# First pair's k and q staged in f32 through the sync queue, with a new table of order and engines

## The chip, the cores and the metric

One NeuronCore of one Trainium2 chip runs the whole program. The metric is the device time of one execution in microseconds; lower is better. Five runs of the kernel before gave 199.79 to 201.91 us with a median of 200.88. The profile is of one further execution, which took 201.26 us.

## The reference

q, k and v are f32 of shape (batch 4, heads 8, 768 positions, head dim 64). Attention looks only at the six best chunks of 32 keys for each query; the result goes through a gated MLP. In short:

```python
k_min, k_max = k_chunks.min(3), k_chunks.max(3)      # 24 chunks of 32 keys
ub = sum(maximum(q * k_min, q * k_max))              # bound per query and chunk
ub = where(causal, ub, -1e9); top_chunks = argsort(ub)[..., -6:]
scores = where(selected and causal, scale * q @ k.T, -1e9)
attn = softmax(scores); x = attn @ v                 # heads side by side: 512 wide
h = relu(x @ w_in); u, v = halves of h
v_n = (v - mean(v)) / sqrt(var(v) + 1e-6)
v_s = w_spatial @ v_n + b_spatial
out = (u * v_s) @ w_out
```

## The kernel before

The heads are worked in 16 pairs (two heads of 64 fill the 128 partitions), four pairs to a batch. For each pair:

- *Load.* k, q and v come from DRAM by DMAs that POOL issues. They cast from f32 to f16 on the way, into `kp`, `qs` and `vt`. The k and q of the first pair come in halves, one head each (lines 364 and 369).
- *Prepare* (`prep_ops`, and `prep_first` for pair 0). k is transposed to `kT`, either by TensorE with a copy out of PSUM, or by a transposing DMA on SP's queue. VectorE takes maximum and minimum over each chunk (`t`, then `kmm`). Copies spread these into `km`, and `kT` into `kh`. q is transposed on TensorE and split in its positive and negative part (`rq`). A matmul of `rq` and `km` gives the bounds (line 475). VectorE masks, takes the eight best, and writes a selection beside q in `qs`. That is transposed to `a`, by TensorE or by a transposing DMA (line 502).
- *Attend.* The score matmuls (line 627) take `kh` and `a`. The exponential on ScalarE writes `e` (line 637). The causal diagonal is masked by an added matmul or by POOL. The matmul with v (line 653) is followed by a normalisation into `x16` and a transpose into `xT`.

After four pairs the MLP of a batch runs: v and u (lines 699 and 726), the normalisation, the spatial matmul (740), the gate `g`, its transpose `gT`, the output matmul (761), a copy `o`, and a store on SP's queue.

`Schedule.op` records every operation with the engines that may do it, what it reads and writes, and for some a choice: `s.choice` names two alternatives, of which the plan takes one, as for a transpose on TensorE or by DMA. The order isn't found when the program is built. The string `PLAN` holds three characters for each operation: which one, on which engine, and in which PSUM bank its result goes. `Schedule.run` reads it and emits the operations in that order. Each engine then takes its own instructions strictly in that order, and so do the queues of SP and POOL: an instruction whose input isn't there holds all that stand behind it. All matmul results share eight PSUM banks.

The cost figures beside an operation (`("POOL", 0.81, 0)`) belong to the search that wrote the table; the program doesn't act on them.

Of the kernel before, what the change touches and what calls it, by code (L numbers as in the profile page):

```python
# [8 lines left out]
F32 = mybir.dt.float32  # L9
# [5 lines left out]
P = 128  # L15
# [20 lines left out]
def blocks(groups):  # L36
# [13 lines left out]
    "0A00600400500300700D00200F00Q00H00C00E00000900a00c00B00100I00L00d00f40K10+82600P10G01AC0g00/00i0"  # L50
    "0b00O01003Q00h00N00q02804k00M00o10k01201101402701912AG1710rK0j01300m00l01501C11B12B01612D02E0181"
    "0s00J00p11DO1E02F03US0n10t10uW1F02N20v01G02Q20w03R02G00x01H42I03S00y82H03V13X02P22O24oC0e04m03Y0"
    "3Z00803a01I12L22K24l02RG2M21sK8400W01yO0X03lS4p03c03b00z12T11hW2J20V02S01u03n03i11a41nC1p02U84r0"
    "1XG1+01j02V01JK1vC1L03d03e04t04s01UO2W04u01c09O03m01MW1W03g03j11kK3f02X05341x01PO1m01O04v01R03h1"
    "2ZS2b888C5404w04z21Z02a03oK2c01rW4y22jS2rO1T82002uG2l05013k18911e03p05503q02105212g42dS3AC3r03tK"
    "1f02202w05118B04x22t04+02f01g02908503u08D03vG3w035W3GO2i02/S8C03D88602443T04/156K3C03F041C5709P0"
    "25037031062G6486309Q06503xW3I032458043049S4MG8E066O3405909S84B09T02oCAi03+48G03z039S3K03L04PK8F0"
    "6702q04UW4O04n04a84R09V05DC4005E05BG5C10T04JO4c08PK8J02n44CC2y05QG8H03M09W04L046S8K08I05j84W08Q0"
    "4E08M10U04804XO8R05l09X05S05TK4TW8SCC005IS4Z02z05K09Z02+09Y05L48T09a09j89f145G4G00R05oO9h14e00S0"
    "68S8U09e09l04H08V09k05N05F44I09d08ZC8a05V08N15uK8O15q05H05d84f05gO5f0Aj08XG5W49b28L05Y0691Ak05PC"  # L60
    "4g0Am88Y0FA0C109c25a05r45b06AW5i09mG5t094SAn05w03OO4i89C45c09n09R03P06B18cC9509o05nK5y09g15z09p0"
    "9q05+0A+09i1Ap09D0A/18fO99WAq0C208g08704j0C4S6Y48+G8iO8d06iK60C6109A08j0Ar06EW8/0C516OO9186F06P0"
    "8tGB02As06Z06G08qC6JS6K0At09206a0Au0C70FB0C808nW8k0C90CB08r0Aw08u06Q16H0CA09F8Az1B14B30Ay0Ax06j0"
    "Av18o06dO9G0A0C9wG6I06L0A8WB20A10AI89x0CH18v0CC0AOSAP06M0FG0FC0B44B506CC6D06k0B606e0CLGCN0A5S6vC"
    "6w0A906sKGU0AJ06/W0Z0B70FI06f0CG16x0CE0AT86R0CM16N06S09z4A60CF0B80AWOAX06t0FH09+0700CD06u0COC6g0"
    "ALG8lSFJ06yOFK06b06z0CP09H0Ho0AU0960FM0CQ06+097475KAM06T06l06U00Y0J60CR08w06h0FL0AB8AC0AZOAa0760"
    "72G9I06c06V0770730A20710BtCBc8Bu0BEOBF0A3KGV0AQ06m06n09J07406W09K0AD08x0Bd0ARW6o0AE08y06X0FQ16p0"
    "BnCAF0AG07cOFN0FO0Bo07I4BqGFVSBr0Ab0Ac0CJ1BP8CS0BiC7d0Bj06r0FX0FW1BHGCK1CI17J0BI078KAd0FU26q0Ga0"
    "790BQ0FP0FYCBfSBg0FR1BKG7K0Ae0BL07e0FT1FS1CYWGW0FZ0D087A0Fa0CZ0CeSD107L0CjG7S4Fb0CmCAl0Gb0Hu07f0"
    "Ck0Gn1CpW7B0Gd07T0Cn07m87U0C30Cq0BSOCf0Fc0Go0CbGCwCHp0BM0Bk07V0DBKHw0BT07n0Hv0Cc0BVWBW09MS7W0CzO"  # L70
    "Gf0C+0Cx0Bv0Gc0Ge0Gg0Gj1Gp4Gl1BlGD5WGi1BX07C0Gr0Bw0Gq1Hx07wO7x0DC0Hq09N0BNCBx0BY07o0Cr0Hz0Hy07M0"
    "Cg0D60BZ0FtKGL4D8WBa0GM07y0Gk0Gh0Fu0ChSD90Cs0Gs4G7CAf0H+0I42By0GFKFlWFm0GG0Ct0Cu0I207ZGGt0DD0Gu0"
    "Gv07a0D20FwSD3WDE07FKG80FiGMG0DF0Fx0DG0G44DIC7p0B+WI7SDJ07z0JA8DoC7G0DPKJ80G50Gw0FD0Fo4GAOGm1B/0"
    "JB1I90DQ0J70GIW7H0Dp0Fj0DR1JE0GB0Dy8Dz0E8GDS0DKOJD0I01I61I81JG0DL0H3KI31JF0H/0Fp0Dq0FzSGJ0De4DM0"
    "D+1Hr0I51HHCMM0JI0I10IAWGC0MI0HI0JH0HZ8JK0E90H40GN0Ha0Df0Dg0HEODN0IB0IC0DUCJM2DV0HBKHF0Hc8F+0MH0"
    "EA0ID0GX0HC0H04DO0DW1F/0DX0MO0Hd0H10HOWJJ0JROEBSDjCDk0Dl0JN1GDGJS0HP0JL0H6KGO0IE0MY17g0EC0ED0JT0"
    "JU8MN07+0H70Dh0DY0E2O7P4HJ0E30E40Na0D/CGP0DT0DZ07q0Dm0HUWFq0MP0GQ0JV0Ou0MQ07Q0Dn0HV0JP1E00JW0Dr0"
    "JO0E5SHRKHS0Ds0IiGIj0IQODa0JX0E10E60Nc0Iz4FrWG00E71Di0Dt0Du0Db0MR0I+0Hf881KJQ1MbGDc0Hg0ItSH80H9C"
    "Md0Hh0HW0Mc1Iu0G10Ma17j4Iw8Dv0Dx0Dd0INGIR0EYSHK0EEODw0Ix0IO07R08207t8JY0IVGNg0G20HXWIW0MX1HL0EZ0"
    "IbKIc0MZ1MS0MU1O+0MT1MV1Ea07k1EF0JpGMW07u0HM0Eb0Me4K6KJq0Mf0Mg0Nb0Mh0K70IKCJh8EG0EH0K3SNi0Ji0EOG"  # L80
    "JsKIl8EP0Hi0KE4IL0I/0IoCEiOEQ0Im0Nh0Ow0P00Nj0Nl0J90Nk0Nm0No1Jt0Jk8Ip0Ej0Ek0Mi0K0KKF0ER0Hj0IS0Hk0"
    "Ov0Jl0K40JvCNv4Jw0P20Nx1QE0O/0P10Iq0Ir8JeSEI0GR0Nw0IYGIZ0F0CQC0K10J00Nn0EsWJ10Id0Et0Jf0P40KHGJ20"
    "Np1KB4ITKIe0KC0KI0Jm0P30K80MrSMs0NA8Mu4Mv0P91NDGHl0If0NE0Eu0PDSPF1Jx0P60El0Nr0Nq1Ig0PE0KJ0NB0J30"
    "P82JnONs17b0Mz4Jy0F10M+0Nt2Nu2K9GN3KKK0ELSNG8Ev0N0WNy4Jz0J+0KL0F20N10KM0P50P70PGOKOGNz0N+0NH0N40"
    "QD0KkWN/0ES0KP1PH0QI0Ka8PC2KQKNO4NRGNS0KR0Kb0PI0PJ0KS0Kc0N50KT0KU0KpGKd0Kq0NP0O00F30NLOKl0EM0Ke0"
    "KuKL58Mo4QJ0Kv0MJ0KVSL60KW0Kr07l0L8GQXC830Km0QL0PK0NM0PB1QK0Mp0L70QN0KX0QZ1Kw1QM0QO0L2WL30Kn0QP0"
    "QR0Kx0L40QU1NT0OlOOm0Em0Ew0LE4OXKPA0LF0LG0Oa8Ky0OUSKY0OV0Ob0NI0OiWL90OY0OKOQY0EV4Ec0KZ0OCCNJSQQ0"
    "EN0ON8QS2OfKOL0Og0NU0LA1Kf0O9GKs0EW1OA0Mw0NV0QaONW0Nd0Mx4N60Oj0O6KLBSQb0Kg0PhGPi07v0N70N80Ko0Qc0"
    "LC0Kt0LD0OD0LHWQd0Ox0Pb4Kz0PoGQT0Ki0Pc0LI0Pp0EzSLJ1OO0PzOEfCPQ4Kh0O70OHGOc0Kj0E+1Q08Qe0PTWEpKK+0"
    "OI0OE0OFGPR0OdSEg1F40P+0K/0On0Oo0QF0Eq0OP0Op0QV1E/0Q10Le4PeCPf0OQ0LUOPU0L00NX0Pj0Oq0Q3KQ/8Q40LV0"  # L90
    "QqCR00PuSPv0QW0QnWPWKLf0OR0Pr8L10RHSQo0OS0R6GPs0LW0LoWPw0Lg0RN8RI0PX0Lp0Lq0PY0QvSLX0LKOLL0Qr0RKK"
    "Lh0R70Q50LM0LN0Er0RL0QyCOr0Ly4PZGPk0Pl0Pm0Eh0RO0RP0LY0Qz0LO0Qw0R10QkKQl0RC8R9OPxCQs0Q60Q70Q80M6S"
    "EX0RD0Lr0RA0RE0RWGQtKR20R30R40Rq8RFOM70RQ0RR0Lz0Q90M80LRCRS0RUWRgKM90L+0R+ORV0Rr0Rh0Ri0Rj0RX0R/0"
    "S00Rk0RY0S10RvSLi0LlWRZ0Rw0Rx0Ra0Rs0SHKRbORc0Rd1Re0F7GRf0Ry0SBSLb8LS0Lc0S8CS90L/0Rl0Rz0Ls0Rm0Rt0"
    "SC0SEOLT0S20Ru0SK8SL0Lv4Rn0SD0Ro0Rp0MA0SI0F80S30S40S60SF0S50SQST2GF90S70SM0TC8Lm0Ln0Ld0M00SA0SaW"
    "SR0SS0ST0SuCT30Sb0Lw0Sc0SU0SJ0Sd0Se0Sk4Sv0T40Sw0SNKM3SLx0Sl0Sm0SG0MDOSx0Sy0T50SXWT60Sn0TD0ME0MF0"
    "SO0SP0ShCTE0SY1SZ0SpGM40Si0M50S/4T9OT00TA0Sj0T10TF0THWSq0SrKSs0TB0TI0TJSSt0TK0TL0"
# [20 lines left out]
class Schedule:  # L118
# [7 lines left out]
    def op(self, alts, emit, key, r=(), w=(), take=None, drop=None, load=0.0, tag="", when=None):  # L126

        o = Op()
        o.alts = {e: (occ, vis) for e, occ, vis in (alts if isinstance(alts, list) else [alts])}
        o.emit, o.take, o.n, o.when = emit, take, len(self.ops), when  # L130
        deps = set()
# [47 lines left out]
def pe_cost(ns):  # L179
    occ = sum(n * MM + 0.0027 for n in ns)  # L180
    return occ, occ + 0.22
# [11 lines left out]
def kernel(  # L193
# [11 lines left out]
    nc = tc.nc  # L205
    B, H, S, D = q.shape
# [4 lines left out]
    NQT = S // P  # L211
# [15 lines left out]
    V0 = 0.2  # L227
# [30 lines left out]
    KH = [("DVE", 0.36, 0.44), ("POOL", 0.47, 0.53), ("ACT", 0.41, 0.55)]  # L258
    KM = [("POOL", 0.24, 0.30), ("DVE", 0.18, 0.30), ("ACT", 0.11, 0.26)]

    def ring(n, shape, dt, name):
        return [cp.tile(shape, dt, name=f"{name}{j}") for j in range(n)]
# [14 lines left out]
    v_r = ring(4, [P, 2, NQT, D + 2], F16, "vt")  # L277
    kT_r = ring(2, [P, S], F16, "kT")
# [70 lines left out]

    PAIRB = P * 2 * NQT * D * 2 / 120e3  # L350

    def load_ops(i, key):
        b, hp = divmod(i, HP)

        def view(a):
            return a[b, 2 * hp:2 * hp + 2].rearrange("h (so si) d -> si h so d", si=P)

        def one(a, hi):
            return a[b, 2 * hp + hi].rearrange("(so si) d -> si so d", si=P)

        kp, qs, vt = kp_r[i % len(kp_r)], qs_r[i % len(qs_r)], v_r[i % len(v_r)]
        def load_q(hi, key):
            c0 = D * (1 - hi)
            s.op(("POOL", 0.81, 0), lambda: nc.gpsimd.dma_start(out=qs[:, :, hi, c0:c0 + D], in_=one(q, hi)), key,  # L364
                 w=[("qd", i % len(qs_r), hi)], load=PAIRB / 2, tag=f"ldq{i}")

        if i == 0:
            for hi in range(2):
                s.op(("POOL", 0.81, 0), lambda hi=hi: nc.gpsimd.dma_start(out=kp[:, hi], in_=one(k, hi)), key + 0.2 * hi,
                     w=[("kp0", hi)], load=PAIRB / 2, tag=f"ldk{i}")  # L370
                load_q(hi, key + 0.2 * hi + 0.1)
        else:
            s.op(("POOL", 1.0, 0), lambda: nc.gpsimd.dma_start(out=kp, in_=view(k)), key,  # L373
                 w=[("kp", i % len(kp_r))], load=PAIRB, tag=f"ldk{i}")
            for hi in range(2):
                load_q(hi, key + 0.1)
        s.op(("POOL", 1.0, 0), lambda: nc.gpsimd.dma_start(out=vt[:, :, :, 0:D], in_=view(v)), key + (0.2 if i else V0),  # L377
             w=[("vd", i % len(v_r))], load=PAIRB, tag=f"ldv{i}")

# [37 lines left out]
    def prep_ops(i, key):  # L417
# [3 lines left out]
        bk = Bank("tr")  # L421
# [394 lines left out]
```

## Time and profile before

| | us |
|---|---|
| median of 5 runs | 200.88 |
| lowest and highest | 199.79, 201.91 |
| the profiled execution | 201.26 |
| its span, from first to last instruction | 199.6 |
| TensorE busy (matmuls) | 183.2, 92% of the span |
| VectorE busy | 156.6, 78% |
| ScalarE busy | 151.3, 76% |
| POOL busy (its DMA issues counted) | 121.2, 61% |
| first matmul, first score matmul, start of the last group of matmuls | 4.66, 15.63, 194.20 |

The rows of issued DMAs on the page (operation, count, size of each, median time from issue to landing) that bear on the change:

```profile
out_dram<-o SPq DMA_DIRECT2D x24, 256.0 KB, 2.7
qs<-in_q_dram POOLq DMA_DIRECT2D x32, 96.0 KB, 5.0
...
kp<-in_k_dram POOLq DMA_DIRECT2D x15, 192.0 KB, 5.5
```

The page is read as follows. PE is TensorE's matmuls, PEld its weight loads, DVE VectorE, ACT ScalarE, POOL GpSimd, SP the sync engine; a q behind a name means its queue. Rows of 40 digits give the busy share of 40 equal slices in tenths. In the chain of waits every piece has a start, a length and what it is; a piece that begins with DMA is the time from issue to landing. In the timeline a bracket tells how long an engine sat idle before a row and what ended that.

### The profile page before, as it was taken

What the parts mean: (1) busy time and instruction counts of PE and PEld (TensorE: products, weight loads), DVE (VectorE), ACT (ScalarE), POOL (GpSimd) and SP (SyncE); (2) the same over time, 40 slices, a digit from 0 to 9 for tenths busy, and PEclk for the clock granted to TensorE, in tenths of its full rate; (3) what the DMA queues carried; (4) which work ended last, traced back from release to release, by engine and by line L of the source; (5) the groups of instructions that cost most, each with busy time, mean ns of one, the idle gap of its engine ahead of it and who ended that gap; (6) DMA issues with size and microseconds to landing.
All of it is one profiled execution on the core that took longest, in us unless ns stands there. A gap on an engine that the chain in (4) does not pass through costs nothing.

```text
span 199.6 us, 5295 instructions
## 1 busy us (share of the span) xinstructions
PE 183.2 (92%) x1892; PEld 113.3 (57%) x1892; DVE 156.6 (78%) x563; ACT 151.3 (76%) x322; POOL 121.2 (61%) x207
## 2 busy tenths in 40 slices
PE   0588999999998998699899999999999999999992
PEld 0376888885555556464556556655656575444450
DVE  6786999989799895678799998989798374693540
ACT  4999999999898793678778889988888760673152
POOL 7999999999997974396596785742716340000000
PEclk9999999999999999699999999999999999999999
DMA  6999999999999999699999799999899936044575
GB/s 39 115 143 159 194 140 134 154 165 151 121 164 195 125 116 168 75 94 186 101 177 165 161 103 153 120 170 251 139 189 191 196 86 88 0 131 132 132 239 210
DMA packets 121898, 28.79 MB, mean 144 GB/s; under 512 B 116496, under 2 KB 118800, under 8 KB 121872
## 3 DMA queue, kind: packets, MB, share of 16 engines
q0 software_dynamic: 77216, 12.19, 86.5%
q1 hardware_dynamic: 44656, 16.26, 45.1%
q8 instruction: 15, 0.25, 0.5%
q14 instruction: 11, 0.09, 0.1%
HBM read 24.38 MB, written 6.29 MB: 154 GB/s over the span
## 4 chain that ended last, share of the span: by engine, by line
PE 69%; DMA 17%; ACT 5%; DVE 3%; issue 2%; POOL 2%; POOLq 0%; ACTq 0%; SPq 0%
PE bank L627 15%; PE bank L740 12%; DMA a<-qs 11%; PE bank L761 10%; PE bank L653 8%; PE bank L726 8%; PE bank L699 7%; DMA kT<-kp 3%; DMA kp<-in_k_dram 3%; PE bank L475 2%; PE bank L463 2%; PE bank L511 1%; PE bank L630 1%; PE bank L426 1%; ACT rq L249 1%
## 5 line engine op out<-in xcount | busy, mean ns | idle before, releaser
L637 ACT ACTIVATE e<-bank 128x512 f16<-128x512 f32 (+1 forms) x192 | 92.5, 555 | 12.1 <-PE bank L627 10.3
L627 PE MATMUL bank<-a,kh 128*128 128x512 f16 (+3 forms) x256 | 56.0, 308 | 4.3 <-ACT e L637 2.4
L645 POOL TENSOR_SCALAR_AFFINE_SELECT e<-e 128x384 f16<-128x384 f16 x48 | 26.4, 557 | 25.5 <-ACT e L637 19.3
L740 PE MATMUL bank<-vn,wsT 128*128 128x512 f16 x144 | 38.1, 382 | 0.0
L627 PEld LDWEIGHTS <-kh 128*128 128x128 f16 x256 | 22.5, 98 | 22.0 <-issue 4.3
L653 PEld LDWEIGHTS <-e 128*128 128x128 f16 x672 | 26.7, 98 | 5.6 <-issue 0.6
L653 PE MATMUL bank<-vt,e 128*128 128x65 f16 x672 | 28.8, 194 | 0.0
L364 POOL DMA_DIRECT2D qs<-in_q_dram x32 | 27.1, 851 | 0.0
L744 DVE SCALAR_TENSOR_TENSOR g<-bank,bcol,u 128x512 f16<-128x512 f32 x24 | 17.7, 745 | 10.4 <-PE bank L740 7.0
L726 PE MATMUL bank<-w_in,xT 128*128 128x512 f16 x96 | 25.4, 379 | 0.0
L699 PE MATMUL bank<-w_in,xT 128*128 128x512 f16 x96 | 25.0, 379 | 0.0
L761 PE MATMUL bank<-w_out,gT 128*128 128x512 f16 x96 | 24.1, 379 | 0.0
L241 POOL COPY kh<-kT 64x384 f16<-64x384 f16 x42 | 21.7, 519 | 1.8 <-DMA kT<-kp 0.2
L740 PEld LDWEIGHTS <-wsT 128*128 128x128 f16 x144 | 13.1, 98 | 11.9 <-issue 0.4
L239 ACT COPY o<-bank 128x512 f32<-128x512 f32 x19 | 11.1, 590 | 11.4 <-PE bank L761 9.2
L705 DVE BATCH_NORM_STATS2 st<-vraw 128x6 f32<-128x512 f32 x24 | 16.2, 684 | 3.1 <-ACT vraw L249 2.7
L665 DVE TENSOR_TENSOR x<-bank,rec 128x384 f16<-128x384 f32 x32 | 17.6, 551 | 0.5
L249 ACT ACTIVATE vraw<-bank 128x512 f32<-128x512 f32 x19 | 11.1, 607 | 8.5 <-PE bank L699 8.4
L377 POOL DMA_DIRECT2D vt<-in_v_dram x16 | 16.5, 1029 | 0.0
L241 POOL COPY km<-kmm 64x24 f16<-64x24 f16 x36 | 7.8, 218 | 13.7 <-DVE kmm L441 12.4
L373 POOL DMA_DIRECT2D kp<-in_k_dram x15 | 15.5, 1036 | 0.0
L249 ACT ACTIVATE u<-bank 128x512 f16<-128x512 f32 x20 | 12.0, 610 | 3.7 <-PE bank L726 3.6
(88 smaller groups left out, 275.7 us busy)
## 6 DMA issues: line engine op xcount, KB each, us to landing
out_dram<-o SPq DMA_DIRECT2D x24, 256.0 KB, 2.7
qs<-in_q_dram POOLq DMA_DIRECT2D x32, 96.0 KB, 5.0
vt<-in_v_dram POOLq DMA_DIRECT2D x16, 192.0 KB, 6.2
kp<-in_k_dram POOLq DMA_DIRECT2D x15, 192.0 KB, 5.5
ws_raw<-in_moe_w_spatial_dram POOLq DMA_DIRECT2D x3, 384.0 KB, 7.7
w_in<-in_moe_w_in_dram POOLq DMA_DIRECT2D x4, 256.0 KB, 6.3
w_out<-in_moe_w_out_dram POOLq DMA_DIRECT2D x2, 256.0 KB, 5.7
gT<-g SPq DMA_TRANSPOSE x22, 3.5
```

What stands on the lines that cost most here:

```text
L241: nc.gpsimd.tensor_copy(o, f)
L249: nc.scalar.activation(o, f, func=Act.Relu, scale=sign)
L364: s.op(("POOL", 0.81, 0), lambda: nc.gpsimd.dma_start(out=qs[:, :, hi, c0:c0 + D], in_=one(q, hi)), key, w=[("qd", i % len(qs_r), hi)], lo ...
L627: mm(bs.f32[:, col:col + n], lhsT=kh[:, hi, t * P:(t + 1) * P], rhs=af[:, q0 // P:(q0 + n) // P, :], start=True, stop=not dg)
L637: s.op(("ACT", *act_cost(WIDTHS[g])), lambda g=g, bs=bs, e=e: nc.scalar.activation(out=e[:, BASES[g]:BASES[g] + WIDTHS[g]], in_=bs.f32[:, ...
L645: nc.gpsimd.affine_select(out=o, in_=o, compare_op=Alu.is_ge, fill=0.0, base=0, channel_multiplier=-1, pattern=[[0, 3], [1, P]])
L653: mm(o[:, qi, :], lhsT=e[:, c:c + P], rhs=vt[:, hi, t, 0:D + 1], start=(part == 0 and n == 0), stop=(part == 1 and n == len(bl) - 1))
L699: mm(bk.f32, lhsT=x[:, ko, t * P:(t + 1) * P], rhs=w_in_sb[:, ko, DH:DFF], start=(ko == 0), stop=(ko == NDO - 1))
L726: mm(bk.f32, lhsT=x[:, ko, t * P:(t + 1) * P], rhs=w_in_sb[:, ko, 0:DH], start=(ko == 0), stop=(ko == NDO - 1))
L740: mm(bk.f32, lhsT=wsT[:, si, t * P:(t + 1) * P], rhs=vn[:, si, :], start=(si == 0), stop=(si == NQT - 1))
L744: s.op(("DVE", 0.67, 0.80), lambda t=t, bk=bk, g=g: nc.vector.scalar_tensor_tensor(out=g, in0=bk.f32, scalar=bcol[:, t:t + 1], in1=u_r[nu[ ...
L761: mm(bo.f32, lhsT=gT[:, db, :], rhs=w_out_sb[:, db, :], start=(db == 0), stop=(db == KO - 1))
```

## The change

Three things change in the text of the kernel, and the table is drawn anew.

A ring of eight f32 tiles `stage` is added. Every load becomes a choice: by POOL with a cast on the way, as before, or by SP as f32 into `stage`, one head at a time, with a copy of its own (`CAST`, on POOL, ScalarE or VectorE) into the f16 tile. The keys for dependencies are split by head to match.

```diff
+    CAST = [("POOL", 0.43, 0.50), ("ACT", 0.41, 0.55), ("DVE", 0.47, 0.55)]
+    stage_r = ring(8, [P, NQT, D], F32, "stage")
...
+        def load(name, o, f, key, r, w, cost, share):
+
+            cast, stage = s.choice(("ld", name, i))
+            s.op(("POOL", cost, 0), lambda: nc.gpsimd.dma_start(out=o[0] if len(o) == 1 else o[2], in_=f[0] if len(f) == 1 else f[2]),
+                 key, w=w, load=PAIRB * share if i else 0.0, tag=f"ld{name}{i}", when=cast)
+            for j in range(len(w)):
+                n = self_n[0] % len(stage_r)
+                self_n[0] += 1
+                st = stage_r[n]
+                src = s.op(("SP", 0.45, 0), lambda st=st, j=j: nc.sync.dma_start(out=st, in_=f[j]), key, w=[("st", i, name, j)],
+                           load=PAIRB / 2, tag=f"lh{name}{i}", when=stage, after=staged[n])
+                staged[n].append(s.op(CAST, lambda e, st=st, j=j: copy(e, o[j], st, False), key, r=[("st", i, name, j)],
+                                      w=[w[j]], when=stage))
...
-                s.op(("POOL", 0.81, 0), lambda hi=hi: nc.gpsimd.dma_start(out=kp[:, hi], in_=one(k, hi)), key + 0.2 * hi,
-                     w=[("kp0", hi)], load=PAIRB / 2, tag=f"ldk{i}")
-                load_q(hi, key + 0.2 * hi + 0.1)
+                load(f"k{hi}", [kp[:, hi]], [one(k, hi)], key + 0.2 * hi, [], [("kp", nk, hi)], 0.81, 0.5)
```

The new table takes the second way for five loads: the two halves of k and the two of q of pair 0, whose casts all stand on ScalarE, and the v of pair 15 (two halves, cast on POOL). All others stay with POOL.

The table itself is new from end to end: the order on every engine, the PSUM banks, and the engine of many operations. Counted over the program, before and after:

| rows | before | after |
|---|---|---|
| kp transposes on TensorE (128 columns each) | 48 | 60 |
| x transposes on TensorE | 54 | 42 |
| g transposes on TensorE | 8 | 4 |
| kT, xT, gT by transposing DMA on SP | 7, 7, 22 | 5, 9, 23 |
| a by transposing DMA on SP | 11 | 11 |
| rq, u, vraw on ScalarE | 12, 20, 19 | 9, 16, 15 |
| rq, u, vraw on VectorE | 22, 4, 5 | 25, 8, 9 |
| xT copies on ScalarE, VectorE | 1, 8 | 5, 2 |
| kh from kT on ScalarE, VectorE, POOL | 13, 9, 42 | 15, 3, 46 |
| kh from ex on ScalarE, VectorE | 4, 2 | 2, 4 |

The matmuls of scores, bounds, values and MLP are the same in number and shape.

At the start, SP's order becomes k0, q1, k1, q0 (the digit is the head of pair 0), then bcol. POOL's becomes identity, tri, cmask, then the loads of k of pairs 1 and 2, q of pair 2, k of pair 3, q of pair 1. ScalarE's becomes the table load, two copies of ex, the casts of k0 and k1, one half of kT, the cast of q1, three copies of kh, the cast of q0.

## The prediction

> **What bounds the kernel now.** I read the busy rows of the page first, then the busy times by stretch, the chain of waits, and the timeline at the stalls. The page and the stretches (columns: PE, PEld, DVE, ACT, POOL busy with instruction counts, granted TensorE clock, DMA share, GB/s):
>
> ```profile
> PE   0588999999998998699899999999999999999992
> ...
> 0.00:20.00 20.00, 11.62 (x114) 8.79 (x115) 14.85 (x81) 16.61 (x33) 18.64 (x30) 1.00 1.66 114
> 20.00:50.00 30.00, 29.98 (x475) 23.83 (x473) 28.56 (x121) 29.57 (x67) 28.93 (x48) 1.00 1.74 156
> 50.00:65.00 15.00, 13.86 (x169) 8.65 (x167) 13.81 (x58) 12.92 (x31) 13.40 (x26) 1.00 2.01 161
> 65.00:100.00 35.00, 31.78 (x300) 18.90 (x299) 27.45 (x93) 25.20 (x54) 23.51 (x42) 0.95 1.39 123
> 100.00:165.00 65.00, 65.00 (x685) 38.77 (x683) 55.15 (x182) 53.73 (x116) 36.69 (x65) 1.00 1.29 162
> ```
>
> From 20 to 50 us and from 100 us on, TensorE runs one instruction after another; nothing is won there unless its work shrinks. It idles 8.4 us before 20, 1.1 us in 50 to 65, 3.2 us in 65 to 100, and 3.7 us after its last matmul (195.9). Before 50 us ACT and POOL are full too, so the head isn't TensorE's alone. The chain of waits names the middle stalls (start, length, what):
>
> ```profile
> 45.09 6.85 DMA a<-qs
> 51.98 1.25 PE bank L627 x6
> ...
> 56.09 7.05 DMA a<-qs
> 63.18 0.68 PE bank L627 x3
> ...
> 70.24 6.85 DMA kT<-kp
> 77.15 0.70 issue
> ...
> 86.95 8.39 DMA a<-qs
> 95.47 0.43 PE bank L627 x2
> ```
>
> Four times a transposing DMA on SP's queue lands late. The kT one (pair 10) is the dearest; the timeline tells how:
>
> ```profile
> 77.12 1.41 DVE L435 TENSOR_TENSOR t<-kT 128x384 f16<-128x384 f16 x2 [2.10 <-DMA kT<-kp]
> ...
> 80.55 0.70 ACT L249 ACTIVATE rq<-bank 128x640 f16<-128x640 f16 x1 [3.45 <-DVE rq L253]
> ...
> 81.47 1.08 PE L627 MATMUL bank<-a,kh 128*128 128x256 f16 x5 [2.35 <-ACT e L637]
> ...
> 82.34 1.06 PE L740 MATMUL bank<-vn,wsT 128*128 128x512 f16 x2
> ```
>
> VectorE, in its fixed order, waits for kT; the rq row behind it comes late; ScalarE waits for rq with exponentials behind it that free banks; TensorE waits for a bank. Then two L740 rows take 1.06 us where two at 78.52 took 0.59: the clock has fallen (0.67 granted in 80 to 85).
>
> **The change, part by part.** All sums are against the profiled execution, 201.26 us (span 199.6); the median of the runs shown, 200.88, is 0.4 lower.
>
> *TensorE's work.* Twelve more kp transposes, twelve fewer of x, four fewer of g: minus 4 x 0.055 us (six take 0.34 in the chain) = -0.2 us. No other matmul goes.
>
> *The head.* Today POOL issues first-pair loads at 1.31, 2.26, 3.41 and 5.48; TensorE takes the last q half at 9.70. SP has nothing to do there after bcol. After: SP issues k0, q1, k1, q0 at about 0.8, 1.3, 1.8, 2.3 (bcol's issue took 0.46). No HBM load of f32 of this size is in the trace. Nearest row: a 256 KB output store from the same queue, 2.7 us to land; upper end 5.0, the slowest early load of a pair (kp, 6.29 to about 11.3). I take 2.7, as the queue is empty: k0 at 3.5, k1 at 4.5.
>
> The new cost is four casts. None stands in the trace; the nearest ACT row is kh<-kT, 64x384 in 0.513, at whose length I put each: 2.05 us, all on the most loaded engine of the head. ScalarE today runs without a break from 4.10 to the first a copy at 14.78, ending 15.58, and the first score matmul is at 15.63. After, the identity is first on POOL, so ex is ready near 2.3 instead of 4.1. ScalarE's rows up to the first a copy are then: two kh<-ex (1.66), four casts (2.05), one kT half (0.5, between the kh copy and the 128x768 row), nine kh<-kT (4.6), three kmf (0.6), three kT (2.4), one a (0.8) = 12.6 us, so 14.9 if never starved. Casts start at 4.0, so k0 at 3.5 is hidden; without that cover each us of lateness costs one. VectorE's chain ends about the same time: kT half at 5.9 instead of 6.31, but now three of the four rq are on it before the masks (+2 x 0.48), so its selects gain only 0.3 to 0.7. First score near 15.0: -0.6. POOL drops four loads (3.5 us) and issues kp of pair 1 at about 2.2 instead of 4.48, so later loads are 2 to 3 us earlier; that lets the second head's a and pair 1 follow with less than the 0.7 us wait seen at 17.5. Head in all -1.3; ends -2.5 and +1.5.
>
> Here the skill speaks against the change. DMA: Bandwidth & Descriptors, section Issuing engines are not separate DMA queues, says that issuing from several engines saves only sequencer time, since the same 16 DMA engines move the data; its rule table puts casting loads on GpSimd. By the rule the head gains POOL's issue time at best and pays the casts: about zero net. The rows say issue time is the scarce thing: a q load holds POOL 0.85 us and POOL is busy 18.64 of the first 20. I follow the rows, but only to -1.3.
>
> *The table.* Every queue is reordered. Durations of rows stay; what changes is how much TensorE work lies between what releases a transposing DMA and its user. I added up TensorE's rows in both orders (0.216 us a 512-column matmul, 0.056 a transpose, 0.031 a 65-column one, from the chain).
>
> For a<-qs, from the last ub matmul of the pair to its first score: pairs 5 to 9 before 9.3, 9.0, 11.5, 9.4, 9.5 us; after 10.0, 8.9, 9.9, 9.6, 12.3. Pairs 5, 6 and 9 stalled by about 0.6, 0.8 and 1.0 (start to start, above the matmul's 0.216), so the lead needed is about 9.8 to 10.5. With 10.1 the new leads leave 0.1 + 1.2 + 0.2 + 0.5 + 0 = 2.0 instead of 2.4: -0.4.
>
> For pair 10's kT, from its place in the order to VectorE's first use: 2.1 us before, 9.0 after (pair 9: 3.9 and 7.7); it took 6.85. So VectorE shouldn't block: -2.5 us of stall. With it goes the slow clock: 3.52 us busy at 0.67 is 1.2 us lost. TensorE: Matmul & The Clock Gate, section What's actually happening, has the clock fall to half after an idle window of about 3.4 us. Here an idle of 2.35 us, with gaps before it, came ahead of it. By the rule a 2.4 us stall costs 2.4, by the rows 3.6. I use the rows: -1.2.
>
> *Balance.* Counting moved rows by their durations, ScalarE loses about 4 us (11 fewer rq, u and vraw at 0.6 to 0.7, two fewer kh<-ex; four more xT, four casts) and VectorE gains about 4 (eight more u and vraw at 0.69, three more rq; six fewer xT, six fewer kh). VectorE is at 28.56 of 30 in 20 to 50, so some comes out on the path; from 100 on it has 15% spare. Pair 15's v also goes through SP and two POOL casts, late, where POOL is half idle; xT of pairs 0 and 1 move to SP, with leads of 16 and 10 us. One more g transpose leaves the last batch's PE rows for SP; leads there, 5.6 to 8.6, are as before (5.8 to 6.5), so the tail stays. For balance and for new waits which orders alone can't show I add +2, ends 0 and +5: the four old stalls cost 5 in a kernel with the same number of such transfers.
>
> Sum: -0.2 - 1.3 - 0.4 - 2.5 - 1.2 + 2 = -3.6, so 197.7 against the profiled execution, 197.3 against the median. I say **197.8**, as the head term is the least sure.
>
> **Rivals.**
>
> *The stalls only move* (chance 0.20). For it: eleven a<-qs transfers remain, landing in 6.4 us in the median, 4.6 to 8.4; two leads stay under 10. Against it: pair 9's and 10's leads grew. Then the 3.7 of the kT stall comes back elsewhere and only the head counts: 200.88 - 1.3 = 199.6, or 200.5 with half of it.
>
> *Transposes land later* (0.25, the slower side). POOL issues later loads 2 to 3 us earlier, and they share DMA engines with the transposes. If a<-qs for pairs 5 to 8 lands like the last in the chain (8.39 instead of 6.9), each waits 1.5 more: +6, and 197.8 + 6 = 203.8 at most; with one of the four covered, 202.3. It decides from a landing of about 7.8 us on, where 4 x 0.9 eats the gain. Against it: pair 9's transfer was the only a<-qs above 7.1.
>
> *The loads don't come earlier* (inside the range): f32 halves landing after 5 us put k0 at 5.8, 1.8 after ScalarE wants it; the head goes from -1.3 to about +0.5, the total 199.6.
>
> **Numbers.** The forecast has 0.55, its own range 195.5 to 199.8. Moved stalls 0.20, later landing 0.25. To leave no more than 2 in 10 outside, the range is 195.2 to 202.3. What a measurement of this kernel can tell from no change is about 0.5%: 199.9 to 201.9. Faster: 0.52 of the forecast and 0.11 of moved stalls = 0.63. Same: 0.02 + 0.08 + 0.03 = 0.13. Slower: 0.01 + 0.01 + 0.22 = 0.24.
>
> **What would show it.** Head: the first transposes at about 4.7 and the first score near 15.0; ScalarE waiting for stage ahead of the first cast would show late loads. Table: no VectorE wait for kT over 1 us, no granted clock below 0.9 in a slice after 20 us, and TensorE idle in 50 to 100 at about 2 us instead of 4.4. It is wrong if a<-qs lands after 7.8, if VectorE fills beyond 29 of 30 in 20 to 50 with TensorE waiting for rq or rec, or if TensorE idles after 100, where it has no idle now.

## The result, and the profile after

The changed kernel takes **198.19 us** (median of 41 executions, 195.25 to 201.74), the kernel before 200.93 us beside it (78 executions). The ratio is **0.984**, 95% interval 0.9817 to 0.9863: faster by 1.6%, with the whole interval below 1. Ratios here compare only executions within 1.5% of the fastest of their kernel (20 of the 41, with a median of 197.2 us against 200.5), while medians and spreads are those of all, whose quotient here is 0.986. The forecast was 197.8 in a range of 195.2 to 202.3.

The execution that was profiled with this measurement took 199.22 us, above the median of its kernel, with a last store that took 3.6 us to land where 2.0 is usual; so the lines below come from a second profile of the same, unchanged kernel (`a_again` in the experiments), of an execution of 197.23 us with a span of 195.4. Source lines stand 14 further down than before: scores at L641, `a` by DMA at L516, maximum and minimum of chunks at L449; the staged loads are issued at L376, and their casts show as the copy helper's line, L240.

The page's rows of TensorE and of its granted clock, 40 slices each:

```profile
PE   0579999999999999999999999997999999999992
PEclk9999999999999999999999999999999999999999
```

The busy times by stretch (PE, PEld, DVE, ACT, POOL, clock, DMA share, GB/s):

```profile
0.00:20.00 20.00, 11.93 (x123) 9.36 (x124) 16.03 (x79) 16.77 (x31) 17.43 (x32) 1.00 1.90 153
20.00:50.00 30.00, 29.88 (x475) 23.66 (x472) 27.85 (x125) 29.46 (x65) 27.95 (x48) 1.00 1.76 158
50.00:100.00 50.00, 49.27 (x544) 30.85 (x542) 47.68 (x179) 44.15 (x99) 44.07 (x77) 1.00 2.14 152
100.00:165.00 65.00, 63.80 (x634) 37.02 (x632) 51.40 (x159) 46.03 (x102) 28.79 (x53) 1.00 1.08 145
```

The dips of the middle are gone, and the clock column shows 1.00 in all these stretches (for the first 18 us that isn't the rate at which TensorE works, see below). From 50 to 100 us TensorE is idle 0.73 us, where it was 4.4. What it waited for from 38 to 100 us, before and after (us in total, times, longest):

```profile
PE bank L627 <- ACT e L637: 2.4, 1, 2.4
PE bank L627 <- DMA a<-qs: 2.0, 3, 0.8
```

```profile
PE bank L694 <- DVE x L679: 0.3, 1, 0.3
PE bank L641 <- DMA a<-qs: 0.3, 1, 0.3
```

The wait of 2.4 us behind pair 10's kT is gone, and those for `a<-qs` have shrunk to 0.3. One new dip stands in slice 28, and TensorE idles 1.2 us in 100 to 165, where it had no idle.

Busy time hides part of what is lost: a matmul at half clock counts as busy. So for what follows I took from the trace the time between the starts of neighbouring matmuls, less what their columns take in unbroken stretches (0.055 us for a transpose, 0.213 for 512 columns). That is TensorE's **loss**; with the work and the tail it adds up to the span.

| us | before | changed | difference |
|---|---|---|---|
| 0 to 20, the first matmul's wait counted | 13.67 | 13.42 | -0.25 |
| 20 to 50 | 0.59 | 0.91 | +0.32 |
| 50 to 100 | 7.35 | 1.88 | **-5.47** |
| 100 to 165 | 0.80 | 2.24 | **+1.44** |
| 165 to the last matmul | 0.40 | 0.34 | -0.06 |
| work of all columns | 172.73 | 172.51 | -0.22 |
| last matmul to the end | 4.01 | 4.07 | +0.06 |
| span | 199.56 | 195.38 | -4.18 |

The two profiles differ by more than the medians do (4.0 us of execution time against 2.7): each is one execution out of 6 to 7 us of spread. Of the places, all in all: the middle brought 5.5, a new stall at 132 us took back 1.4, and the head, for which the loads were staged, brought a quarter of a microsecond.

What happened in the head is told by the timeline (start, length, engine, row, the idle before it and what ended that):

```profile
3.85 0.51 ACT L240 CAST kp<-stage 128x384 f16<-128x384 f32 x1
...
5.55 0.51 ACT L240 CAST kp<-stage 128x384 f16<-128x384 f32 x1 [1.19 <-DMA stage<-in_k_dram]
...
7.17 1.02 POOL L370 DMA_DIRECT2D kp<-in_k_dram  x1 [1.25 <-ACT qs L240]
...
16.23 0.58 PE L641 MATMUL bank<-a,kh 128*128 128x512 f16 x1 [0.28 <-ACT a L240]
```

A cast takes what was estimated, 0.51 us. But the second half of k landed 3.6 us after its issue, ScalarE stood 1.19 us for it, GpSimd's next load of k stood 1.25 us (it overwrites pair 0's k tile, whose last transposes come only after the late cast; the releaser named is the cast beside them), and the first score is at 16.23 us, not at 15.0; it was at 15.63.

One part of the head's loss isn't a wait. At first TensorE works at half its later rate, although the page's clock row has a 9 there. Two rows of the same form in `a_again`:

```profile
17.25 0.63 PE L641 MATMUL bank<-a,kh 128*128 128x256 f16 x2
...
19.18 0.38 PE L641 MATMUL bank<-a,kh 128*128 128x256 f16 x2
```

In the first row the two matmuls start 0.213 us apart, in the second about 0.108. The rate doubles at 18.2 us here and at 16.9 us in the profile of the kernel before; between the first score and that moment about 1.0 us is lost by it here, and about 0.5 before. In the nine profiles with the changed kernel's head the moment lies between 16.6 and 18.4 us and the loss up to 20 us between 12.7 and 13.6, against 13.7 in three profiles with the head of before. What sets the moment wasn't tested.

### The profile page after: what moved, and what is told of

Its sections match the earlier page's. It is cut to its first block, busy times and chain, and to the rows that moved or that the text cites. A ratio compares the mean times of both kernels' runs of the same rounds, so it can differ in the third digit from the quotient of the medians.

```text
span 197.5 us, 5292 instructions
## 1 busy us (share of the span) xinstructions
PE 181.3 (92%) x1888; PEld 112.8 (57%) x1888; DVE 158.9 (80%) x568; ACT 148.0 (75%) x317; POOL 118.5 (60%) x207
## 4 chain that ended last, share of the span: by engine, by line
PE 70%; DMA 13%; ACT 7%; DVE 5%; issue 2%; SPq 0%; ACTq 0%
PE bank L641 15%; PE bank L754 13%; PE bank L775 9%; PE bank L740 9%; PE bank L667 9%; DMA a<-qs 8%; PE bank L713 7%; ACT e L651 4%; DMA kp<-in_k_dram 3%; DMA stage<-in_k_dram 2%; PE bank L477 2%; PE bank L489 1%; PE bank L644 1%; PE bank L440 1%; PE bank L525 1%
## 5 line engine op out<-in xcount | busy, mean ns | idle before, releaser
L641 PE MATMUL bank<-a,kh 128*128 128x512 f16 (+3 forms) x256 | 56.6, 308 | 2.2 <-DMA a<-qs 2.1
L659 POOL TENSOR_SCALAR_AFFINE_SELECT e<-e 128x384 f16<-128x384 f16 x48 | 25.6, 550 | 24.7 <-ACT e L651 23.7
L641 PEld LDWEIGHTS <-kh 128*128 128x128 f16 x256 | 22.7, 98 | 17.7 <-DMA a<-qs 2.8
L667 PEld LDWEIGHTS <-e 128*128 128x128 f16 x672 | 25.4, 97 | 4.8 <-issue 0.2
L667 PE MATMUL bank<-vt,e 128*128 128x65 f16 x672 | 27.1, 193 | 0.1
L242 POOL COPY kh<-kT 64x384 f16<-64x384 f16 x46 | 24.1, 524 | 3.8 <-PE bank L641 1.4
L370 POOL DMA_DIRECT2D qs<-in_q_dram x30 | 25.1, 841 | 0.0
L240 ACT COPY o<-bank 128x512 f32<-128x512 f32 x18 | 10.5, 588 | 18.3 <-PE bank L775 18.3
L370 POOL DMA_DIRECT2D vt<-in_v_dram x15 | 15.4, 1024 | 0.0
L775 PEld LDWEIGHTS <-gT 128*128 128x128 f16 x96 | 9.1, 98 | 9.7
L713 PEld LDWEIGHTS <-xT 128*128 128x128 f16 x96 | 9.0, 98 | 9.1
L740 PEld LDWEIGHTS <-xT 128*128 128x128 f16 x96 | 8.9, 98 | 8.5
```

What stands on the lines that cost most here:

```text
L242: nc.gpsimd.tensor_copy(o, f)
L370: s.op(("POOL", cost, 0), lambda: nc.gpsimd.dma_start(out=o[0] if len(o) == 1 else o[2], in_=f[0] if len(f) == 1 else f[2]), key, w=w, loa ...
L641: mm(bs.f32[:, col:col + n], lhsT=kh[:, hi, t * P:(t + 1) * P], rhs=af[:, q0 // P:(q0 + n) // P, :], start=True, stop=not dg)
L659: nc.gpsimd.affine_select(out=o, in_=o, compare_op=Alu.is_ge, fill=0.0, base=0, channel_multiplier=-1, pattern=[[0, 3], [1, P]])
L667: mm(o[:, qi, :], lhsT=e[:, c:c + P], rhs=vt[:, hi, t, 0:D + 1], start=(part == 0 and n == 0), stop=(part == 1 and n == len(bl) - 1))
L713: mm(bk.f32, lhsT=x[:, ko, t * P:(t + 1) * P], rhs=w_in_sb[:, ko, DH:DFF], start=(ko == 0), stop=(ko == NDO - 1))
```

## The experiments

Two theories were to be told apart. **Order**: the gain is that fewer rows stand ahead of their transfers in the table; the staging is incidental. **Staging**: freeing GpSimd's queue at the start is what pays, and the table merely goes with it. All ratios are against the kernel before, run on the same chip in the same rounds. A move in the table is shown by the rows in their order on one engine.

### The two halves of the change, taken apart

`a_again` is the changed kernel once more.

> The changed kernel as it is, once more, so that its stalls can be told from those of one execution. Theory of the order (the gain lies in the middle, where more TensorE work stands ahead of what a transposing DMA feeds): TensorE loses under 3.5 us between 50 and 100 us again, where the kernel before lost 7 in its profile, and the ratio to the kernel before is 0.98 to 0.99. Theory of chance (the profiled executions differed by their DMA landings): stalls of 5 us or more in that stretch.

Measured: ratio 0.9818 (0.9766 to 0.987), 196.21 us. Its loss in 50 to 100 is 1.88 us.

`a_pool` keeps the new table, but pair 0 is loaded by GpSimd with a cast on the way, as before:

```diff
-SP:   stage<-k0, stage<-q1, stage<-k1, stage<-q0, bcol
-ACT:  cast k0, cast k1, cast q1, cast q0 among the copies
+SP:   bcol
+POOL: k, k, q of pair 0 ahead of pair 1's k, the other q half behind it
```

The identity and the masks, too, go back behind these loads on GpSimd, as in the kernel before.

> The changed kernel with pair 0's k and q loaded by POOL with a cast, in the kernel before's POOL order (k0, k1, identity, q1, kp of pair 1, q0, kp of pair 2, masks), no staging, no ScalarE casts for them; the rest of the table as changed. Theory of the order: the staging is worth little, since the first score was no earlier with it; the ratio to the kernel before stays 0.98 to 0.99, within 1 us of the changed kernel. Rival, the staged loads carry the gain: ratio 0.995 or more.

Measured: ratio 0.9946 (0.9895 to 0.9998), 200.2 us: without staging the new table keeps about a third of the gain. Where it is lost is told by what TensorE waited for from 0 to 50 us in `a_pool` (us in total, times, longest):

```profile
PE bank L544 <- DMA kp<-in_k_dram: 5.1, 2, 4.4
PE bank L439 <- DMA kp<-in_k_dram: 2.9, 3, 1.2
...
PE bank L476 <- DMA qs<-in_q_dram: 0.6, 2, 0.3
PE bank L439 <- DVE rec L674: 0.5, 1, 0.5
PE bank L488 <- POOL km L241: 0.4, 1, 0.4
PE bank L666 <- DMA vt<-in_v_dram: 0.3, 1, 0.3
```

The head's own loss rises by 0.5 us only (13.42 to 13.91). The larger part is behind it: 3.06 us instead of 0.91 in 20 to 50. (In 50 to 100 it loses 1.0 more, and after 100 it loses 1.3 less, since the stall at 132 us isn't there.) GpSimd's queue has hardly a gap there (28.3 of 30 us busy), so four more load issues at its front (0.81 to 1.03 us each) stay in it: the two halves of pair 5's q are issued at 28.62 and 31.76 us instead of 26.52 and 29.72, and q, v and `km` each arrive a little after TensorE wants them.

`b_stage` is the opposite: the kernel before with the staged loads and the casts on ScalarE, and otherwise its own table.

```diff
-POOL: k, k, q of pair 0, pair 1's k, the other q half of pair 0
+POOL: pair 1's k
-SP:   bcol
+SP:   stage<-k0, stage<-q1, stage<-k1, stage<-q0, bcol
+ACT:  cast k0 ahead of the copies of ex, casts k1, q1, q0 among them
```

> The kernel before with pair 0's k and q staged in f32 by SP (k0, q1, k1, q0) and cast on ScalarE (k0 first, then two ex copies, k1, q1, two ex copies, q0); the rest of its order unchanged. Theory of the order: four casts of 0.51 us go on ScalarE, which is full until the first score, so the head doesn't gain; ratio 0.997 to 1.008. Rival, the staged loads carry the gain (POOL gives up four issues, 3.5 us, and its later loads come earlier): ratio 0.985 to 0.993.

Measured: ratio 1.0082 (1.0041 to 1.0123), 201.57 us. Staging put into the old table costs. TensorE's waits from 0 to 50 us in `b_stage`:

```profile
PE bank L540 <- ACT kp L239: 6.0, 2, 4.2
PE bank L585 <- ACT kmf L239: 2.1, 1, 2.1
```

ScalarE, with two us of casts in an order that wasn't made for them, hands over `kmf` 2.1 us late, and the first score comes at 16.94 us. The old table has no waits for loads in 20 to 50 (loss 0.59), so GpSimd's freed time finds nothing to shorten. The profile, of the fastest of the twelve executions, loses 1.1 us more than before up to 20 us and 0.5 more in 20 to 50, but 2.6 less in 50 to 100, so its span is no longer than before's. That staging costs here rests on the twelve times; where the cost arises in most executions isn't shown.

So neither theory holds alone. The table without staging gives 0.5%, staging without the table -0.8%, both 1.6 to 1.8%: the two need each other. The likely reason is that the new table fills the time that staging frees on GpSimd, as the losses of `a_pool` in 20 to 50 us say. A better place for the casts in the old table, or for the four loads in the new one, wasn't tried.

### The middle: which rows made it

`b_kt` is the kernel before, with VectorE's two rows that read pair 10's kT moved back behind other work that is ready:

```diff
 DVE:
-t<-kT pair 10 (x2)
 kmm, t, km, rq of pair 9
+t<-kT pair 10 (x2)
```

> The kernel before with two rows moved: VectorE's first two reads of pair 10's kT stand behind pair 9's kmm, km and rq rows instead of ahead of them; nothing else. Theory of the order: VectorE no longer blocks on pair 10's kT with pair 9's rows behind it; the 2.5 us stall near 79 us and the half clock after it go, together 3.7 in the profiled execution, and the time falls by 1.5 to 3.7 us (ratio 0.982 to 0.993). Rival, the stalls only move: TensorE waits as long at another place, ratio 0.995 to 1.005. Rival, the staged loads carry the gain: also 0.995 to 1.005.

Measured: ratio 0.9959 (0.9923 to 0.9995), 199.1 us: less than expected, and within what the rivals expect. VectorE's wait for kT and the half clock are gone, but TensorE's loss in 50 to 100 fell only from 7.35 to 5.40 us. The timeline shows what had stood behind:

```profile
78.16 0.59 PE L740 MATMUL bank<-vn,wsT 128*128 128x512 f16 x2
80.41 0.67 PE L627 MATMUL bank<-a,kh 128*128 128x256 f16 x5 [1.66 <-DMA a<-qs]
...
93.71 0.43 PE L627 MATMUL bank<-a,kh 128*128 128x512 f16 x2 [1.74 <-DVE st L705]
```

At 80.41 it is pair 8's transpose `a<-qs`, issued at 71.57 us, landing 8.8 us later. The line at 93.71 names VectorE, which is misleading: its row ended at 93.71, but it has nothing that a score reads; pair 9's `a<-qs` was issued at 84.56 and landed 9.0 us later, at 93.6. Each transpose took 2.4 and 0.6 us longer than in the profile of before.

`b_lead` gives these two the lead that they need, too:

```diff
 PE:
-scores of pair 8 (2 rows)
 score of pair 7, s, A*V of pair 7 (2 rows)
+scores of pair 8 (2 rows)
...
-scores of pair 9 (3 rows)
 v, bounds of pair 10, u, v
+scores of pair 9 (3 rows)
```

> The kernel before, with pair 10's two kT rows of VectorE moved back as in b_kt, and besides with the first two score rows of pair 8 and the first three of pair 9 (with their exponentials) moved behind 1.1 and 1.5 us of other TensorE work, so that the two transposes a<-qs on which b_kt still waited (issued 71.6 and 84.6 us, landing 8.8 and 9.0 us later) have that much longer. Theory of order (the middle of the kernel is lost to rows that stand ahead of their DMAs, and nothing else): both waits shrink by their added lead, from 1.8 and 1.9 us to below 0.9 each; TensorE's excess in 50 to 100 us falls from 5.4 to about 3.2 us, the time from 199.1 to 197.0 us, ratio to before 0.980 to 0.988. Rival (the work behind, the exponentials and ScalarE, is what is short, so that a score moved back makes its own wait): the excess stays above 4.5 us and the ratio at 0.993 to 0.999.

Measured: ratio 0.9881 (0.9837 to 0.9925), 198.63 us. The loss in 50 to 100 is 3.20 us, as expected; the ratio is just above the 0.988 that order allowed. Three moves of a few rows thus give the old kernel 1.2%, most of what the whole change gives. Not expected was the other side: TensorE lost 1.6 us at 103.8, waiting for gT. The three gT transposes issued from 96 to 100 us took 6.0 to 7.1 us, where they took 3.8 to 4.8 in `b_kt`. They stood among `a`, kT and several loads, as they did there; what slowed them wasn't tested.

`a_kt` puts the bad order into the good table: VectorE's first read of pair 10's kT is moved ahead, as the old table had it.

```diff
 DVE:
+t<-kT pair 10 (m=1)
 mask, max8, qs of pair 8 and nine other rows
-t<-kT pair 10 (m=1)
```

> The changed kernel, with VectorE's first read of pair 10's kT moved ahead of pair 8's mask row, to about 70 us, some 3 us before the landing at 73.2: the order of the kernel before in this one place. Theory of order (a VectorE row that stands ahead of its transpose holds what is queued behind it, and TensorE follows): VectorE waits 2 to 3.5 us there, TensorE's excess in 50 to 100 us rises from 1.9 to 4 us or more, the time by 2 to 4 us, to a ratio of 0.992 to 1.002 against before. Rival (VectorE has room there, about 30% idle, and the wait is made good): under 1 us, a ratio of 0.980 to 0.987.

Measured: ratio 0.9928 (0.9877 to 0.9979), from five of twelve executions: worse than the changed kernel by 1.1%, within what order expects. The median of all twelve is 201.85 us, against 201.55 for the kernel before beside it, so the cost may be larger. The loss in 50 to 100 us is 6.8, where 4 or more was expected. VectorE's and TensorE's waits in 65 to 80 us of `a_kt` (us in total, times, longest):

```profile
DVE t L449 <- DMA kT<-kp: 5.1, 1, 5.1
...
PE bank L641 <- DVE qs L511: 4.3, 1, 4.3
```

One row that stands before its transfer costs VectorE 5.1 us, and TensorE 4.3 of them, through the selection (`qs`) queued behind it: VectorE had no room to make it good. The wait is longer than the 2 to 3.5 us expected, in part since kT took 8.3 us to land in this profile and 7.0 in `a_again`. The kernel before had the same wait, shorter (2.1 us) and reaching TensorE by another chain, through `rq` and the exponentials; it is what the table took out.

### The new stall at 132 us

In the changed kernel pair 13's `a<-qs` is issued at 125.2 us and lands 8.1 us later; GpSimd issues two vt loads at 124.7 and 125.7. `a_vt13` sends these two some 8 us later; their readers come after 144 us.

```diff
 POOL:
-vt pair 14, vt pair 13
 km (2), mask, km, kh, mask
+vt pair 14, vt pair 13
```

> The changed kernel, with the two vt loads that GpSimd issues at 125.1 and 126.2 us, beside pair 13's transpose a<-qs (issued 125.7, landing 8.2 us later, TensorE waiting 1.3 us at 132), issued 7 us later instead, behind the mask rows at 132.7 us; their first readers come after 144 us. Theory that the loads slow the transpose: it lands in 5.5 to 6.5 us, the stall at 132 us is gone, time 1.0 to 1.5 us shorter than the changed kernel, a ratio of 0.973 to 0.978 against before. Rival (the transpose is slow for its neighbours on its own queue, a store and gT, or by itself): landing 7.5 us or more, the stall within 0.4 us of what it was, no gain.

Measured: ratio 0.9839 (0.9792 to 0.9886), 198.17 us. The landing of this one transpose, in the changed kernel and in `a_vt13` (the view of one source line, window around it):

```profile
DMA to landing us min/median/max: 8.1/8.1/8.1
```

```profile
DMA to landing us min/median/max: 3.8/3.8/3.8
```

The mechanism is shown: with the two loads out of the way it takes 3.8 us, here and in `a_all` below, and the stall is gone (loss in 130 to 140 us 0.12 instead of 1.4). In between lie `a_kt`, `a_pool` and `a_lead13`, whose tables issue the same loads and the same transpose, but the loads 0.3 us ahead of it and 0.7 behind instead of 0.5 and 0.5: it lands after 6.5 to 6.6 us. In `a_kt` and `a_pool` that was early enough for the stall to be gone with the loads where they were. Yet no time was gained: a ratio of 0.973 to 0.978 was expected. The profiled execution of `a_vt13` had a wait of 2.9 us for pair 5's q load at 37 us, well ahead of the edit, so its span can't be set against the others'; `a_all` below tells more.

`a_lead13` leaves the transfers alone and moves pair 13's scores behind 1.3 us of other TensorE work:

```diff
 PE:
-scores of pair 13 (5 rows), between the following
 v, A*V of pair 12, bounds of pair 15, A*V of pair 12
+scores of pair 13 (5 rows)
```

> The changed kernel with its transfers as they are, and pair 13's first five score rows (with two of their exponentials) moved behind 1.3 us of other TensorE work (a half of v, two A*V halves and the selection matmul of pair 15). Its transpose a<-qs landed 8.1 to 8.2 us after its issue in four profiles, and TensorE waited 1.3 to 1.6 us for it at 132 us. Theory that the wait is a lead that is too short by its own length, and nothing behind is short: TensorE's excess in 130 to 140 us falls from 1.4 to 1.8 us to 0.2 to 0.5, nothing appears in 140 to 165 (0.4 us now), and the time is 0.9 to 1.4 us below the changed kernel's, a ratio of 0.973 to 0.980 against before. Rival (as in a_all: what is taken out there is given back, here because the exponentials come later and A*V waits for them): the excess over 130 to 165 us stays above 1.5 us, a ratio of 0.980 to 0.986.

Measured: ratio 0.987 (0.9808 to 0.9931), 198.01 us. The loss in 130 to 140 us is 0.60 us, where it was 1.4 to 1.7 with the stall, and from 140 to 165 nothing is added (0.1 us in each 10); but the time isn't shorter. This profile doesn't test the lead: the transpose landed after 6.5 us, and with such a landing `a_kt` loses 0.11 there without the edit. `a_best` below, with the same edit and a landing of 7.6 us, loses 0.59, so the longer lead does take most of the stall away, and costs some 0.5 us of its own. Its profiled execution, too, had a disturbance ahead of the edit: pair 6's `a<-qs` was waited for 2.9 us at 60 us. Whether the edit is worth its 1 us can't be read from medians that are uncertain by 0.5%.

### The head, and the edits together

`a_order` issues the staged loads in the order in which ScalarE casts them:

```diff
 SP:
-stage<-k0, stage<-q1, stage<-k1, stage<-q0
+stage<-k0, stage<-k1, stage<-q1, stage<-q0
```

> The changed kernel, with the four staged loads issued in the order k0, k1, q1, q0 instead of k0, q1, k1, q0. In its trace k1 landed at 5.88 us and ScalarE waited 1.53 us for it. Theory that the head is set by k1's landing: k1 lands at 4.6 to 5.2 us, ScalarE's wait falls below 0.9 us, the first score comes 0.5 to 1 us earlier than 16.47, and the time falls by 0.4 to 1 us, a ratio of 0.975 to 0.980. Rival (the head is set by what comes behind: q1, which now lands later, and GpSimd's second k load at 9.95 us): the first score within 0.3 us of 16.47, or later, a ratio of 0.981 to 0.985.

Measured: ratio 0.9817 (0.9765 to 0.9868), 197.37 us, equal to `a_again`. ScalarE's wait for k1 fell from 1.19 to 0.47 us, as expected, but the first score is at 16.05 us, only 0.2 earlier than in `a_again` (0.4 earlier than the 16.47 from which both expectations counted), and the loss up to 20 us is 13.31 instead of 13.42. The rival is nearer: k1 alone isn't what sets the head. Behind it TensorE waits 1.1 us for pair 1's k, which GpSimd loads, and ScalarE's next copy of kT waits for that: 0.88 us instead of 0.46.

`a_q5` issues the second half of pair 5's q load 2.4 us earlier:

```diff
 POOL:
 q pair 5, first half
+q pair 5, second half
 w_in, kh, kh, kh
-q pair 5, second half
```

> The changed kernel, with the second half of pair 5's q load issued right behind the first half on GpSimd, ahead of a w_in load and three kh copies: at about 27.4 instead of 29.8 us; the rows that use it come at 36.9 us. In the profile of a_vt13 this load took 9.4 us to land (5.3 to 5.8 us in the profiles of the changed kernel) and TensorE waited 2.9 us for it, with its clock halved after. Theory that the changed kernel's spread (195.3 to 201.7 us in 41 executions) is this load landing late in part of them: no wait for it in the profile, and no time above 199.5 us; the median is 196 to 197.5 us, a ratio of 0.972 to 0.981 against before. Rival (the spread comes from elsewhere, or the whole stretch's loads are late together and the wait passes to the next one): times as spread as before, a ratio of 0.981 to 0.986.

Measured: ratio 0.9813 (0.9754 to 0.9873), 197.71 us, times of 196.24 to 199.6. No wait for the load, but the ratio is the changed kernel's, and six executions are too few to say that the long ones are gone. Undecided.

`a_all` combines `a_order`, `a_vt13` and `a_q5`.

> The changed kernel with three edits at once: the staged loads in the order of a_order, pair 13's and 14's vt loads 7 us later as in a_vt13, and pair 5's q load 2.4 us earlier as in a_q5. Theory that each removes a wait of its own (0.3 us at the first score, 1.3 us at 132 us, 3 us in part of the executions at 37 us): TensorE's excess over 50 to 165 us falls from 4.4 us to below 3.2, the time to 194.5 to 196.5 us, a ratio of 0.966 to 0.977 against before, better than both kernels. Rival (a wait taken out of the middle is given back later, since VectorE and ScalarE are as far behind): a ratio of 0.979 or more.

Measured: ratio 0.979 (0.9697 to 0.9883), 198.72 us. The theory asked for 0.977 or less; the interval, which rests on two executions, holds both cases, and by the medians of all the time is no shorter. The profile is clearer. The 1.3 us at 132 us are gone, and 2.0 us are lost at 148.8:

```profile
150.09 1.29 DVE L244 COPY o<-bank 128x512 f32<-128x512 f32 x2 [2.79 <-DMA out_dram<-o]
...
150.83 0.53 PE L667 MATMUL bank<-vt,e 128*128 128x65 f16 x12 [1.83 <-DVE o L244]
```

The vt loads, moved to 133 us, now stand beside gT transposes, stores and the staged v. Three of the four gT there took 5.9 to 8.8 us, against 3.0 to 4.7 in `a_again`, and a store issued at 135.6 took 6.6 us against 2.5. VectorE waits for a store to free its `o` tile, and TensorE for the bank that this copy drains. That is the rival's outcome, by another way than it named: the traffic is moved, not removed.

`a_best` combines `a_order`, `a_q5` and `a_lead13`, which move no transfers into others.

> a_lead13 with the staged loads in the order of a_order and pair 5's q load 2.4 us earlier as in a_q5, without the later vt loads of a_all, whose traffic came back on the gT transposes and stores behind. Theory: each edit took a wait away without adding traffic anywhere, so the gains of a_lead13 (0.9 to 1.4 us) and some 0.3 us of the head add: 194.5 to 196.5 us, a ratio of 0.969 to 0.978. Rival (only a_lead13's wait was on the path of most executions): equal to a_lead13 within 0.4%.

Measured: ratio 0.9852 (0.9803 to 0.9901), 197.49 us, its six times between 196.38 and 198.06. Its profile has the shortest span of all, 194.5 us. What TensorE waited for from 100 to 165 us in it, in full:

```profile
PE bank L641 <- ACT e L651: 0.3, 1, 0.3
```

Its losses are 13.06 up to 20 us, 0.87, 2.26, 1.43 and 0.33: 0.8 us under `a_again` in all: 0.4 less in the head and 0.8 less after 100 us, 0.4 more in the middle. The head's part isn't the edit's: the first score comes later, at 16.58 us, but TensorE's rate doubles at 17.0 us instead of 18.2. By the medians it is no faster than the changed kernel. A version that beats both kernels was not shown.

## Why the prediction was right, and where it wasn't

The time and its sign were right, and so was the main reason. That the sum came out so near is partly luck: two terms were off in opposite directions, the head by 1 us and the middle by 1.4. By its own steps, with the losses of the table above:

- *TensorE's work*, -0.2: 172.73 to 172.51, right.
- *The head*, -1.3: **-0.25 measured; this is the mis-sized term.** Its first part, the first score 0.6 us earlier, went the other way: 0.6 us later (0.3 of that is more work done ahead of it). ScalarE's rows up to the first `a` copy last 12.7 us, as summed (12.6), but "14.9 if never starved" failed: ScalarE waited 1.19 us for k1 and 0.46 for pair 1's k. "I take 2.7, as the queue is empty" held for the first staged load alone, which took 2.8 us; the three behind it took 3.3, 3.6 and 4.1. Cover was asked for k0 only, which had it (its cast starts at 3.85); k1, put at 4.5, landed at 5.5. And "later loads are 2 to 3 us earlier" took the issue for the landing: `a_order` takes most of the wait for k1 away, and pair 1's k then holds ScalarE instead. Pair 1's k, from the view of the line of GpSimd's loads in `a_again`:

```profile
DMA to landing us min/median/max: 6.3/6.3/6.3
```

  It is issued at 2.13 instead of 4.48 us and takes 6.3 us instead of 4.1, so it lands at 8.4 instead of 8.6. Six loads were under way at once. The second part, -0.7 behind the first score, came to -0.5 in spite of the half rate, which lasts 1.4 us longer than before. In the number, the rule that was weighed and not followed (the Trainium skill, DMA: Bandwidth & Descriptors, Issuing engines are not separate DMA queues: issuing from another engine saves only issue time) was nearer: "about zero net" against 0.25 measured. The issue time that it does save is what `a_pool` prices at some 2 us, but in 20 to 50 us, not at the first score, where I had looked for it.
- *a<-qs leads*, -0.4, *kT*, -2.5, *the clock*, -1.2: -4.1 in all, -5.5 measured. The kT step is confirmed from both sides, by `b_kt` and `a_kt`. In the new table kT is there before VectorE asks, and no slice after 20 us is below full clock. The leads were worth more than 0.4. The sum itself was uneven: it set 2.0 us, reckoned with a need of 10.1, against 2.4 measured; with 10.1 the old leads leave 3.2, which makes the term -1.2. And with the leads of the new table only 0.3 us of waits remained (0.9 in the other profile of the changed kernel), not 2.0. From the other side, `b_kt` shows that of the kT stall's 3.7 only 2.0 was had while pair 8's and 9's transposes stood at their old leads of 9 to 9.5 us. I had added the stalls as if each could be removed by itself. They stood one behind the other: when the first is taken away, the next is reached earlier. (In that profile the two transposes also landed 2.4 and 0.6 us later after their issue, which may be part of it.)
- *Balance and new waits*, +2: +1.8 (0.32 in 20 to 50 and 1.44 in 100 to 165). The size was right; that TensorE would idle after 100 us was named as a sign against the forecast. It does, for 1.2 us, almost all of it at one place, where two loads are issued beside the transpose.
- *The tail*, 0: +0.06.
- *VectorE at its limit* in 20 to 50: 27.85 of 30, under the 29 that would have spoken against the forecast.

Of the rivals, "transposes land later" was right about the mechanism in one place of eleven: 8.1 us at pair 13, above the 7.8 from which it was to count; the others land in 4.1 to 7.3. "The loads don't come earlier" held in what it says of the landings, with the head at -0.25, not at +0.5. "The stalls only move" describes `b_kt` and `a_all`, not the change; half of its head term makes 200.2, not 200.5.

What stays open: the changed kernel's executions lie between 195.3 and 201.7 us, and part of the long ones may come from a transfer that lands late at random, as pair 5's q load in the profile of `a_vt13` (9.4 us instead of 5.3 to 5.8). Its stretches before and at that wait, columns as above:

```profile
30.00:36.00 6.00, 6.00 (x120) 5.17 (x118) 5.48 (x27) 5.97 (x16) 5.68 (x11) 1.00 1.86 133
36.00:40.00 4.00, 1.07 (x15) 0.65 (x12) 1.33 (x4) 1.54 (x4) 2.59 (x8) 1.00 4.42 90
```

The DMA engines' busy share more than doubles while they move a third less: packets took longer, with no more of them asked for. `a_q5` was made for this load and doesn't settle whether it makes the spread.

## What to carry to other kernels

In a kernel with a fixed order on every engine, look for each row that stands ahead of its transfer, and count the work between issue and first use against the slowest landing in the trace, not the median; three moves of that kind gave some two thirds of what the whole change did. Taking load issues off a full queue paid, in this kernel, over the stretch in which that queue had hardly a gap, not where the loads are used, and only with an order that used the time. Before a transfer is moved, look at what it will stand beside: in `a_all` the time it took from its neighbours went to its new ones.

## What the hardware showed that wasn't expected

- A transposing DMA of one shape (`a<-qs`), from one queue, took 3.8 to 9.4 us in these profiles, and what runs beside it is part of the reason. Pair 13's took 7.6 to 8.2 us with two vt loads of 192 KB issued 0.5 to 0.8 us before and 0.2 to 0.5 after it, 6.5 to 6.6 with the loads 0.3 before and 0.7 after, and 3.8 with the loads out of the way.
- Four f32 loads of 192 KB issued from one queue within 1.7 us land after 2.8, 3.3, 3.6 and 4.1 us. GpSimd's first load of a whole pair, issued among them, takes 5.6 to 6.3 us (`b_stage`, `a_order`, `a_again`), and 4.1 to 4.3 without them (before, `a_pool`); the loads that GpSimd issues behind it also follow sooner there, so the lengthening isn't due to the four alone.
- The clock fell to half (granted 0.66 to 0.88 in the stretches of 5 us at the end of the wait or behind it) after single TensorE waits of 2.35 us (before), 2.9 us (`a_vt13`, `a_lead13`) and 4.3 us (`a_kt`), and not after 1.7 us (`b_kt`) or 1.8 us (`a_all`).
- At the start TensorE works at half rate in every profile, until 15.7 to 18.4 us, and the granted clock on the page doesn't show it: two 256-column matmuls start 0.213 us apart before that moment, 0.108 behind it.
